# Linear attention and a feed-forward layer on one core: all tokens of k and v in five chunks instead of four chunks and a rest

## Chip, cores and metric

The kernel runs on one core of one Trainium2 chip. The metric is the device time in microseconds (us) of one execution, lower is better. Before the change it was 295.58 us (median of 3 runs, 295.31 to 296.41). Times of a kernel are compared with runs of the kernel before on the same chip. A run is called slow when it is more than 1.5% above the fastest of its kernel, and slow runs are left out of ratios; the medians and ranges quoted take in all runs.

## The reference

```python
# q, k, v: 8 batches, 8 heads, 576 tokens, 64; w_in 512 x 2048; w_out 2048 x 512; all float32
phi = lambda x: np.where(x > 0, x, np.exp(x) - 1.0) + 1.0
kv  = einsum('bhsd,bhse->bhde', phi(k), v);  z = sum over s of phi(k)
att = (phi(q) @ kv) / (phi(q) @ z + 1e-6)                  # per batch and head
x   = att as (8*576, 512);  out = gelu_tanh(x @ w_in) @ w_out
```

576 tokens don't divide into blocks of 128 partitions: 4 x 128 leave 64. How those 64 are treated is what changes.

## The kernel before

A batch's 512 main tokens are loaded as four chunks ("main"); the 64 others ("rest") of two batches share one tile of 128 partitions. So q, k and v have a main and a rest path each. Loads and DMA transposes are issued by SyncE (SP), the rest loads mostly by GpSimd (POOL).

```python
pld   = ctx.enter_context(tc.tile_pool(name="pld", bufs=6))    # staged float32 loads, one tag
...
psm = ctx.enter_context(tc.tile_pool(name="psm", bufs=2))      # transposed q of the rest
px  = ctx.enter_context(tc.tile_pool(name="px", bufs=5))       # attention output x, before its transpose
...
    def load_main(src, b, name, eng, parts=1):
        t = pld.tile([P, H, C * D], FP32, name=name, tag="ld")
...
        # five matmuls for each pair of heads: four main chunks, then the rest
        for c in range(C):
            nc.tensor.matmul(dst, lhsT=kp[:, c, ...], rhs=vps[b % 2][...], start=(c == 0), stop=False)
        nc.tensor.matmul(dst, lhsT=kr[:, 0, ...], rhs=vrs[...][...], start=False, stop=True)
...
    def plan_rest(m, j0, j1):
        def tq():
            box["qt"] = psm.tile([P, NP, P], BF16, name="qtr")
            nc.sync.dma_start_transpose(out=box["qt"], in_=phi["qr", m]...)
        def nab(): ...          # reads box["qt"], makes x, transposes x into xt_rest on SP
        at(*j0, tq); at(*j1, nab)
...
    plan_rest(1, (2, 2, 8), (1, 3, 14))
    for m in range(2, 4):
        at(1, 2 * m - 2, 9, lambda m=m: load_rests(m, (("qr", q),)))
    for m in range(2, 4):
        plan_rest(m, (2, 2 * m - 2, 9), (1, 2 * m, 14))
```

The program is laid out by hand in slots (half, stage, slot); every engine runs its own instructions in that order. The transpose of q's rest m=1 is placed at (2, 2, 8) and that of m=2 at (2, 2, 9), next to each other, and the first is read only much later.

## Time and profile before

| | before |
|---|---|
| time, median | 295.58 us |
| span of the profiled run | 293.4 us |
| TensorE (PE) busy | 285.2 us, 97% |
| first matmul of the feed-forward layer | 20.33 us |
| data moved by DMA in the first 60 us | 21.09 MB |
| all DMA traffic | 53.23 MB |

TensorE sets the time; what can cost time is whatever makes it wait. Two views matter for what follows and are not in the prediction. The first shows busy time of each engine in stretches, with the granted clock, the busy share of the DMA engines and GB/s as the last three numbers:

```profile
12.00:20.00 8.00, 6.63 (x77) 4.86 (x74) 5.93 (x17) 4.98 (x11) 2.16 (x3) 1.00 1.08 384
20.00:30.00 10.00, 9.85 (x67) 6.33 (x69) 6.19 (x9) 8.08 (x13) 5.26 (x6) 1.00 1.06 391
```

The columns after the length of the stretch are PE, PE's weight loads, DVE, ACT and POOL. Between 12 and 30 us the DMA engines are full (1.08 and 1.06) and move 384 and 391 GB/s. PE works 9.85 of the 10 us from 20 to 30.

The second is the timeline of SP's queue around 110 us: start, duration of the issue, line, what.

```profile
106.55 3.66 SPq L522 DMA_TRANSPOSE xt_rest<-x  x1
111.71 6.79 SPq L463 DMA_TRANSPOSE qt<-q_p  x4
118.55 2.63 SPq L512 DMA_TRANSPOSE qtr<-qr_p  x2
122.69 7.17 SPq L498 DMA_TRANSPOSE xt<-x  x4
```

One queue carries the transposes of q of batch 4, then those of two rests of q, then those of x, one behind another. The division that needs the first of them runs at 121.26 without a wait.

### The profile page before, as it was taken

To read this page: it belongs to the slowest core of one execution; us is meant where nothing else is said; L and a number is where in the kernel's file an instruction comes from. 1 tells how busy PE (TensorE), PEld (TensorE's weight loads), DVE (VectorE), ACT (ScalarE), POOL (GpSimd) and SP (SyncE) were. 2 spreads that over 40 slices of the span, in tenths; PEclk is the share of its full clock that TensorE was granted. 3 is DMA by queue.
4 is the path that set the end of the run, shared out by engine and by line. 5 is a ranking of instruction groups with operands and counts; after the bars stand their busy time and mean duration, and the time that the engine had idled before them with its cause. 6 is when DMAs were issued, how large, how long until landed. Compare 5 with 4: busy or idle time off the path is not lost.

```text
span 293.4 us, 4220 instructions
## 1 busy us (share of the span) xinstructions
PE 285.2 (97%) x1669; PEld 149.2 (51%) x1698; DVE 114.3 (39%) x189; ACT 158.6 (54%) x221; POOL 36.0 (12%) x56
## 2 busy tenths in 40 slices
PE   8989999999999999999999999999999999999995
PEld 6865456644565544544454445544554444444443
DVE  3676426236486683356125652543231000000002
ACT  4539943679965772567255935682560176017400
POOL 8045458400005200000000000000000000000000
PEclk9999999999999999999999999999999999999999
DMA  7999999994599899539914797304231110021032
GB/s 233 317 373 401 398 365 387 333 365 141 150 344 247 179 283 294 159 61 287 307 64 72 251 306 127 71 3 139 75 60 31 71 71 2 0 96 47 2 72 72
DMA packets 64259, 53.23 MB, mean 181 GB/s; under 512 B 31728, under 2 KB 57584, under 8 KB 64240
## 3 DMA queue, kind: packets, MB, share of 16 engines
q1 hardware_dynamic: 60816, 41.82, 51.1%
q10 hardware_dynamic: 2464, 8.52, 7.8%
q0 software_dynamic: 960, 2.62, 3.1%
q8 instruction: 13, 0.21, 0.3%
q14 instruction: 6, 0.05, 0.0%
HBM read 36.70 MB, written 9.44 MB: 157 GB/s over the span
## 4 chain that ended last, share of the span: by engine, by line
PE 91%; DMA 3%; DVE 3%; issue 1%; SPq 0%; ACT 0%; DVEq 0%
PE h_ps L309 42%; PE o_ps L727 40%; DMA q_x<-in_q_dram 3%; PE n_ps L261 3%; PE kv_ps L227 3%; PE o_ps L696 1%; PE t_ps L284 1%; DVE x L273 1%; DVE kvbd L250 1%; PE kv_ps L234 1%; SPq L67 0%; ACT q_e L168 0%; PE t_ps L255 0%; DVE xt L391 0%; DVE q_p L185 0%
## 5 line engine op out<-in xcount | busy, mean ns | idle before, releaser
L727 PE MATMUL o_ps<-w_out_sb,g 128*128 128x512 bf16 x547 | 123.4, 379 | 0.8 <-issue 0.2
L309 PE MATMUL h_ps<-xt,w_in_sb 128*128 128x512 bf16 (+1 forms) x534 | 118.6, 364 | 0.8
L684 ACT ACTIVATE g<-h_ps 128x512 bf16<-128x512 f32 x144 | 83.7, 602 | 46.6 <-PE h_ps L309 44.9
L727 PEld LDWEIGHTS <-g 128*128 128x128 bf16 x560 | 54.2, 98 | 62.6
L309 PEld LDWEIGHTS <-w_in_sb 128*128 128x128 bf16 x612 | 57.6, 97 | 54.7 <-issue 0.5
L742 ACT COPY o_sb<-o_ps 128x512 f32<-128x512 f32 x18 | 10.5, 585 | 57.8 <-PE o_ps L727 57.8
L740 DVE COPY o_sb<-o_ps 128x512 f32<-128x512 f32 x17 | 11.7, 688 | 64.5 <-PE o_ps L727 57.2
L273 DVE TENSOR_TENSOR x<-n_ps,r 128x512 bf16<-128x512 f32 x36 | 24.9, 691 | 1.2
L250 DVE CAST kvbd<-kv_ps 64x260 bf16<-64x260 f32 (+1 forms) x16 | 6.6, 410 | 39.5 <-PE kv_ps L234 39.4
L168 ACT ACTIVATE k_e<-k_x 128x2048 bf16<-128x2048 f32 (+1 forms) x9 | 15.5, 1721 | 4.7 <-DMA k_x<-in_k_dram 4.6
L168 ACT ACTIVATE q_e<-q_x 128x2048 bf16<-128x2048 f32 (+1 forms) x10 | 15.5, 1557 | 3.5 <-DMA q_x<-in_q_dram 3.5
L271 DVE RECIPROCAL r<-n_ps 128x8 f32<-128x8 f32 x36 | 7.4, 205 | 24.1 <-PE n_ps L261 24.1
L185 DVE TENSOR_TENSOR k_p<-k_p,k_e 128x2048 bf16<-128x2048 bf16 (+1 forms) x9 | 10.5, 1172 | 13.3 <-ACT k_e L168 13.2
L336 PE MATMUL w_ps<-warm 128*128 128x252 bf16 x94 | 13.8, 312 | 1.2 <-DVE warm L127 1.1
L309 PE MATMUL h_ps<-xt_rest,w_in_sb 128*128 128x512 bf16 x62 | 13.9, 379 | 0.1
L261 PEld LDWEIGHTS <-qt 128*128 128x128 bf16 x128 | 9.7, 98 | 7.9 <-issue 1.0
L211 DVE CAST vp<-v_x 128x2048 bf16<-128x2048 f32 (+1 forms) x9 | 9.3, 1042 | 11.0 <-DMA v_x<-in_v_dram 11.0
L261 PE MATMUL n_ps<-kvbd,qt 128*128 128x130 bf16 x128 | 12.7, 221 | 0.6 <-ACT kvbd L250 0.2
L179 DVE TENSOR_SCALAR q_p<-q_x 128x2048 bf16<-128x2048 f32 (+1 forms) x10 | 10.6, 1064 | 6.7 <-DMA q_x<-in_q_dram 6.5
L227 PEld LDWEIGHTS <-k_p 128*128 128x128 bf16 x128 | 9.6, 96 | 6.2 <-DVE vp L211 0.8
L227 PE MATMUL kv_ps<-vp,k_p 128*128 128x130 bf16 x128 | 11.8, 220 | 0.5 <-DVE vp L211 0.5
L336 PEld LDWEIGHTS <-warm 128*128 128x128 bf16 x94 | 10.4, 113 | 3.4 <-DVE warm L127 1.1
(52 smaller groups left out, 140.3 us busy)
## 6 DMA issues: line engine op xcount, KB each, us to landing
out_dram<-o_sb ACTq DMA_DIRECT2D x16, 512.0 KB, 4.9
k_x<-in_k_dram SPq DMA_DIRECT2D x7, 1024.0 KB, 5.9
v_x<-in_v_dram SPq DMA_DIRECT2D x7, 1024.0 KB, 12.1
q_x<-in_q_dram SPq DMA_DIRECT2D x6, 1024.0 KB, 8.6
w_st<-in_moe_w_out_dram SPq DMA_DIRECT2D x4, 1024.0 KB, 11.1
w_st<-in_moe_w_in_dram SPq DMA_DIRECT2D x3, 1024.0 KB, 8.6
q_x<-in_q_dram SPq DMA_DIRECT2D x4, 512.0 KB, 10.0
k_x<-in_k_dram SPq DMA_DIRECT2D x2, 512.0 KB, 4.2
```

The costliest lines, as they stand in the source:

```text
L168: nc.scalar.activation(e[:, :, hs, :].rearrange("p c h d -> p h c d"), by_chunk(x[:, hs]), AF.Exp)
L179: nc.vector.tensor_scalar(xp[:, :, hs, :].rearrange("p c h d -> p h c d"), by_chunk(x[:, hs]), 1.0, 1.0, op0=ALU.add, op1=ALU.max,)
L185: nc.vector.tensor_tensor(xp[:, :, hs, :], xp[:, :, hs, :], e[:, :, hs, :], op=ALU.min)
L227: nc.tensor.matmul(dst, lhsT=kp[:, c, P * i : P * (i + 1)], rhs=vps[b % 2][:, 2 * i : 2 * i + 2, c, :], start=(c == 0), stop=False,)
L261: nc.tensor.matmul(n_ps[rows, i // 2, 2 * E * (i % 2) : 2 * E * (i % 2) + 2 * E], lhsT=qt_c[:, i, rows], rhs=kvbd[:, i, :], skip_group_che ...
L273: nc.vector.tensor_tensor(x, n_v[:, :, :, 0:D], r[:, :, :, None].to_broadcast([P, 2, 4, D]), op=ALU.mult,)
L309: nc.tensor.matmul(h_ps[:, tok], lhsT=w_in_sb[:, c, P * m : P * (m + 1)], rhs=xt[:, c, tok], start=(c == 0), stop=(c == KM - 1), skip_grou ...
L336: nc.tensor.matmul(w_ps[:, 0:252], lhsT=warm[:, 0:P], rhs=warm)
L684: nc.scalar.activation(gs[j][:, i, :], ps, AF.Gelu_apprx_tanh)
L727: nc.tensor.matmul(o_pss[t], lhsT=g[:, m, P * t : P * (t + 1)], rhs=w_out_sb[:, m, :], start=(m == 0), stop=(m == MM - 1),)
L740: nc.vector.tensor_copy(dst, o_ps)
L742: nc.scalar.copy(dst, o_ps)
```

## The change

The intent: the rest path of k and v goes away. All 576 tokens of k and v are laid out in five chunks: even partitions take five of nine consecutive tokens, odd ones four. The fifth chunk of the odd partitions is filled with zeros and masked in phi(k). That removes the 256-byte rest loads of k and v and their small instructions, and keeps 160 matmuls of the same shape. q keeps its rest. To make room (the fifth chunk makes load tiles 10,240 bytes per partition instead of 8,192), two rings lose a buffer.

```diff
-    psm = ctx.enter_context(tc.tile_pool(name="psm", bufs=2))
-    px = ctx.enter_context(tc.tile_pool(name="px", bufs=5))
+    psm = ctx.enter_context(tc.tile_pool(name="psm", bufs=1))
+    px = ctx.enter_context(tc.tile_pool(name="px", bufs=4))
...
+    def load_kv(src, b, name, parts=1, fill=nc.gpsimd):
+        t = staged(name, LD).rearrange("p (h x) -> p h x", h=H)
+        for i in range(parts):
+            s = slice(i * hs, (i + 1) * hs)
+            fill.memset(t[:, s, C * D :], 0.0)
+            x = src[b, s].rearrange("h (r n) d -> r h (n d)", n=2 * C + 1)
+            nc.sync.dma_start(out=t[1:P:2, s, 0 : C * D], in_=x[:, :, CK * D :])
+            nc.sync.dma_start(out=t[0:P:2, s], in_=x[:, :, 0 : CK * D])
...
-    vps = [const.tile([P, H, C, E], BF16, name=f"vp{i}") for i in range(2)]
-    vrs = [ ... four tiles [P, H, E] ... ]
+    even = const.tile([P, 1], FP32, name="even")
+    vps = [const.tile([P, H, CK, E], BF16, name=f"vp{i}") for i in range(2)]
...
+            nc.vector.scalar_tensor_tensor(          # phi_min, fifth chunk
+                xp[:, C, hs, :], xp[:, C, hs, :], even, e[:, C, hs, :],
+                op0=ALU.mult, op1=ALU.min)
...
-        for c in range(C):  ... stop=False;  then the matmul of the rest, stop=True
+        for c in range(CK): ... stop=(c == CK - 1)
...
-        at(2, 2 * m - 3, 3, lambda m=m: load_rests(m, (("kr", k), ("vr", v))))
-        at(1, 2 * m - 2, 9, lambda m=m: load_rests(m, (("qr", q),)))
+        at(1, 2 * m - 2, 9, lambda m=m: load_rest(m, nc.gpsimd))
```

Cut: the removed helpers of the rests of k and v, the same edits in the prologue, and batch 3's load, which moves behind the first rest loads.

## The prediction

> **What bounds the kernel now.** I read the page from the top: part 1 (busy time), then the groups by line for the instructions that the change touches, then the chain that ended last in order of time, then the timeline of the first 20 us.
>
> ```profile
> span 293.4 us, 4220 instructions
> PE 285.2 (97%) x1669; PEld 149.2 (51%) x1698; DVE 114.3 (39%) x189; ACT 158.6 (54%) x221; POOL 36.0 (12%) x56
> ...
> L227 PE MATMUL kv_ps<-vp,k_p 128*128 128x130 bf16 x128 | 11.8, 220 | 0.5 <-DVE vp L211 0.5
> ...
> L234 PE MATMUL kv_ps<-vr,kr_p 128*128 128x130 bf16 x32 | 7.0, 218 | 0.0
> ```
>
> PE works 97% of the span; DVE, ACT and POOL have 179, 135 and 257 us to spare. The work that the change merges is the last two rows: four matmuls over main chunks plus one over the rest for each of 32 pairs of heads, 160 in all. Five chunks make 32 x 5 = 160 matmuls of the same shape. So the bound engine gets no work and loses none.
>
> Busy time of PE is modelled, so I checked it by pitch in the chain:
>
> ```profile
> 2.34 9.05 DMA q_x<-in_q_dram
> ...
> 12.50 0.69 DVE q_p L185
> 13.19 0.34 DVE kr_p L179
> ...
> 13.97 0.41 DVE vr L219
> 14.38 0.33 DVE qt L345
> 14.71 0.35 DVE vp L211
> ...
> 174.60 1.73 PE h_ps L309 x8
> ```
>
> Columns: start, us, what. Eight 512-column matmuls take 1.73 us, 216 ns each, back to back. Between 145 and 235 us PE is busy 14.89 to 14.95 of each 15 us that I cut. What is left to win is only where the chain is not PE: the first 20 us (q's loads until 11.39, then ACT, DVE, small matmuls), a DVE eviction of about 0.9 us at 46.2, a copy of 0.4 us at 53.5, and some 3 us of last copies and stores.
>
> The first matmul of the MLP starts at 20.33 us. What leads there:
>
> ```profile
> 0.83 0.16 DVE L127 MEMSET warm<- 128x126 uint32 x1 [0.83 <-PEq L787]
> ...
> 1.06 10.63 PE L336 MATMUL w_ps<-warm 128*128 128x252 bf16 x72 [1.06 <-DVE warm L127]
> ...
> 11.53 0.61 PE L344 MATMUL t_ps<-ident,q_p 128*128 128x128 bf16 x8
> ...
> 13.25 0.64 PE L344 MATMUL t_ps<-ident,q_p 128*128 128x128 bf16 x8
> ...
> 14.30 0.41 DVE L345 COPY qt<-t_ps 128x512 bf16<-128x512 bf16 x1
> 14.31 1.25 ACT L211 CAST vp<-v_x 128x512 bf16<-128x512 f32 x2
> ```
>
> Two things end together here: the data of q (second half landed 11.39) and PE's own queue of 72 warming matmuls, which is issued to its end just when the first half of q is ready. PE takes them in order, so nothing of q can be transposed before the 72 are through.
>
> **What the Trainium skill says.** "TensorE: Matmul & The Clock Gate", Part 1: the array starts at half rate and a free-running window of 3.4 us must be busy before it runs at full rate. The trace agrees in kind: until about 7.0 us the warming matmuls come roughly every 0.21 us (252 columns), afterwards every 0.107 us. It means that a later start of them costs a cold matmul's worth less than its delay. "VectorE: DVE Perf Modes", Zero memsets can be issued as uint32: a memset takes one cycle per element whatever the type. 126 words took 163 ns here, which fits one cycle at 0.96 GHz plus some 30 ns. "DMA: Bandwidth & Descriptors", Specifications: 512 B is the minimum for line rate. The rest loads have 256 B runs; the trace agrees: while the two of the prologue are in flight (9 to 11 us) the engines are full (share 1.16 and 1.14) but move 192 and 260 GB/s, against 354 at 7 to 8 us and 376 at 12 to 13. The same page, Rules for kernel authors, says of two transfers to disjoint partition halves that they serialize on the same 16 engines and gain nothing. A pair for odd and even partitions is that; no run here shows its price yet.
>
> **The change, part by part.**
>
> Bytes: five chunks of 9 tokens in 128 partitions are the 576 tokens, so the same bytes in 1280 B and 1024 B runs. Each k or v load becomes two issues of half the descriptors. On SP an issue of 512 KB took about 0.5 us, one of 1024 KB 0.91 us, so it goes by descriptors and two halves cost one whole.
>
> Steady state, per batch (durations by shape, the slope from the 1024 and 2048 forms). ACT: exp of k goes from 2048 to 2560 elements, 512 x 0.83 ns = +0.43, less half a rest exp, 0.61/2 = -0.31: +0.12 us. DVE: line of phi 512 x 0.51 = +0.26, the masked minimum of the fifth chunk, estimated at one element a cycle, +0.60, cast of v +0.26; less half of a rest line (0.42), of a rest minimum (0.43) and of two rest casts (0.84): -0.84. Sum +0.28 us, some 2 us in all on an engine 39% busy. POOL: twelve rest issues of 0.69 us go (8.2 us), and 14 fills of 512 elements come, estimated 0.6 to 1 us each. All lies beside PE: 0.
>
> Early middle, 20 to 66 us, where DMA is full (share 1.05 and over): v of batch 1 lands at 42.85, its cast ends at 44.1 and PE takes it at 44.80, 0.7 us of slack. The bytes ahead of it are the same, with less in 256 B runs: not later. The even half of k of batch 2 must now wait for a fill that stands on POOL behind the cast of the third piece of w_out (ends 42.1). A backlog until 45.4 (the fourth piece landing) hides that. Batch 3 is asked for at about 50 us instead of 46; 3.4 MB for batch 2, then 3.4 MB for batch 3 at 0.38 MB/us: done near 66 us, wanted near 75. The rings of x (5 to 4) and of the rest's q (2 to 1) are reused only several slots later. Nothing on the path: 0.
>
> Prologue. (a) Removed from the chain: the kr and vr work on DVE between 13.19 and 14.38. It cannot all be won: the copy of qt after it needs the transposes, done at 13.9, so it is worth 0.4 us. (b) Added: DVE does four fills of 256 floats before it clears the tile of the warming matmuls. 256/0.96 + 30 = 0.30 us each, about 1.1 us together. The warming starts at 2.1 instead of 1.06; by 7.0 us it has done 23 instead of 28, so it ends at about 7.0 + 49 x 0.107 = 12.2 us; at 12.7 if the clock opens a full delay later. Transposes of the first half then at 12.3, ten more warming matmuls that stand in the program between the two halves (1.07), transposes of the second half from about 13.8 (now 13.25), copy of qt on DVE from 14.5 (now 14.30). (c) ACT loses a rest exp (0.61), but its third copy waits for that later transpose, then come two casts of v with 640 elements, 0.72 us each instead of 0.62: the second ends near 16.2 instead of 15.56. The last pair of kv needs it: +0.35 to +0.7 us by the time kv is complete, after which the rest of the chain is the same. (d) q: 131 KB of k are now ahead of it, +0.35 us at 370 GB/s, against the 256 B loads no longer crowding it. It may land from 9.5 to 11.8; either way PE's queue, through the second half's transposes near 13.8, hides it (11.8 + 1.07 + 0.69 = 13.6).
>
> Sum: 0 in the steady state, about +0.4 us in the prologue.
>
> **The rivals.** First, that the prologue gets faster: q and v land up to 2 us earlier without the 256 B loads, and the DVE chain is shorter. For it: the dip of GB/s above. Against: the warming queue in front of the transposes. If the fills take half of my figure, it would be 295.58 - 0.5 to - 1.0, about 294.8. Second, that strided half loads run slower, or use the engines unevenly: from 20 to 66 us DMA is the resource without slack, v of batch 1 has 0.7 us of it. At 10% lower rate that load (some 40 us of full DMA) comes 3 to 4 us late and PE waits 3 us: 299. Against: both halves spread over the whole of the partitions, with runs of 1 KB or more. Third, a POOL fill that blocks an in-order queue, so that a load misses its slot: 1 to 2 us, about 297; my slacks of several us speak against it.
>
> **Range and chances.** 295.58 + 0.4 = 296.0, say 295.9, as the first rival is likelier than the second. Three runs before spread over 1.1 us. The two prologue readings give 294.8 to 296.6; with the spread 294.5 to 297.4. Within 2% means 289.7 to 301.5: faster would need 5.9 us out of 8.2 us in which PE idles at all, mostly start and end; slower needs the second rival in full force.
>
> **What would show it.** Right: 160 kv matmuls in one group, PE busy within 1 us of 285, first MLP matmul at 20.5 to 21.2 us, warming from about 2.1, the rest of the chain unbroken at 216 ns. Wrong: warming from under 1.6 us and the first MLP matmul before 20.0 (first rival); PE waiting at kv of batch 1 for the cast of v (second); DVE or ACT waiting for k or v of batches 2 to 7 with PE idle behind them (third).

## The result, and the profile after

After the change the time is 309.53 us (median of 4 runs, 306.24 to 310.15), before 295.44 beside it. The ratio is 1.045 (95% interval 1.037 to 1.053): slower. Ratios here are the mean time of one kernel's fast runs over that of the other's of the same rounds, so they are not quite the ratio of the medians quoted.

The page of the changed kernel, top lines:

```profile
span 307.2 us, 4256 instructions
...
PE 288.4 (94%) x1669; PEld 149.6 (49%) x1698; DVE 115.7 (38%) x185; ACT 159.7 (52%) x216; POOL 32.1 (10%) x49
```

PE's busy time rose by 3.2 us only, with the same 1669 instructions; the span rose by 13.8. So nearly 11 us are idle time of PE, and the rest is slower clock. The waits of PE, as total, number and longest in us:

```profile
PE n_ps L251 <- DMA qt<-q_p: 6.8, 2, 4.3
PE w_ps L323 <- DVE warm L135: 2.1, 1, 2.1
PE kv_ps L224 <- DVE vp L214: 1.5, 2, 1.0
PE o_ps L696 <- POOL w_out_sb L162: 0.7, 1, 0.7
PE h_ps L299 <- ACT g L653: 0.6, 1, 0.6
```

The first line is new and the largest: twice PE stands still for a transposed q. Where the loss arises, by comparing starts of the same matmuls in the two traces:

| PE reaches | before | after | later by |
|---|---|---|---|
| first feed-forward matmul | 20.33 | 20.75 | 0.4 |
| second block of h | 53.92 | 55.96 | 2.0 |
| output of stage 2 | 103.05 | 106.23 | 3.2 |
| output of stage 3 | 130.59 | 139.92 | 9.3 |
| output of stage 4 | 160.79 | 174.46 | 13.7 |

So there is a small early loss of 3 us and then two jumps of 6.2 and 4.3 us. The early part, by stretches:

```profile
12.00:20.00 8.00, 6.57 (x82) 5.20 (x81) 5.64 (x14) 4.97 (x9) 1.36 (x2) 1.00 1.07 364
20.00:30.00 10.00, 9.15 (x68) 5.80 (x67) 5.40 (x8) 7.13 (x10) 4.71 (x5) 1.00 1.05 369
```

The DMA engines are as full as before (1.07, 1.05) but move 364 and 369 instead of 384 and 391 GB/s. Full engines that move less are the first sign that each byte has become dearer, not that less is asked for. In the first 60 us 19.81 MB are moved instead of 21.09.

SP's queue at the first jump:

```profile
111.43 5.66 SPq L496 DMA_TRANSPOSE xt_rest<-x  x1
117.18 9.24 SPq L438 DMA_TRANSPOSE qt<-q_p  x4
126.53 13.67 SPq L486 DMA_TRANSPOSE qtr<-qr_p  x2
140.30 2.52 SPq L472 DMA_TRANSPOSE xt<-x  x2
```

The four transposes of q take 9.24 us of issue, 6.79 before, and land after 11.67. The two of q's rest take 13.67, 2.63 before: the second waits for its only buffer, which the first division of a rest gives free at about 139. Everything behind it in the queue, x first of all, is 17.6 us later than before. POOL's queue just ahead of that:

```profile
113.18 0.53 POOL L88 MEMSET v_x<- 128x512 f32 x1 [5.43 <-issue]
113.71 1.49 POOL L97 DMA_DIRECT2D q_r<-in_q_dram  x2
```

The last rest load of q, issued at 95.58 before, now stands behind fills that wait for a free load tile, and is issued at 113.71, straight into the transposes. PE, with its idle time in brackets:

```profile
128.90 0.41 PE L251 MATMUL n_ps<-kvbd,qt 128*128 128x130 bf16 x4 [4.29 <-DMA qt<-q_p]
...
129.84 2.77 PE L299 MATMUL h_ps<-xt,w_in_sb 128*128 128x512 bf16 x6 [0.22 <-issue]
```

After the stall six matmuls take 2.77 us, 462 ns each instead of 216: the granted clock is 0.50 from 130 to 132 us. That is 1.5 us more, so the stall of 4.3 us costs about 5.8 of this jump's 6.2 us.

The second jump holds a stall of the same kind:

```profile
163.49 0.62 PE L251 MATMUL n_ps<-kvbd,qt 128*128 128x130 bf16 x4 [2.55 <-DMA qt<-q_p]
```

The transposes that it waits for are issued at 154.07 us, 139.93 before, as they stand behind the delayed part of SP's queue. Here too the granted clock is 0.50 afterwards, from 164 to 166 us.

### The profile page after: what moved, and what is told of

Same layout as the page of the kernel before. It is cut to its first block, busy times and chain, and to the rows that moved or that the text cites. A ratio compares the mean times of both kernels' runs of the same rounds, so it can differ in the third digit from the quotient of the medians.

```text
span 307.2 us, 4256 instructions
## 1 busy us (share of the span) xinstructions
PE 288.4 (94%) x1669; PEld 149.6 (49%) x1698; DVE 115.7 (38%) x185; ACT 159.7 (52%) x216; POOL 32.1 (10%) x49
## 3 DMA queue, kind: packets, MB, share of 16 engines
q0 software_dynamic: 384, 1.05, 1.6%
## 4 chain that ended last, share of the span: by engine, by line
PE 74%; DMA 16%; DVE 3%; SPq 2%; issue 2%; POOL 1%; ACT 1%; DVEq 0%
PE o_ps L696 35%; PE h_ps L299 31%; DMA qt<-q_p 7%; DMA w_st<-in_moe_w_in_dram 4%; PE n_ps L251 3%; DMA w_st<-in_moe_w_out_dram 3%; DMA q_x<-in_q_dram 2%; PE kv_ps L224 2%; SPq L91 1%; PE o_ps L665 1%; SPq L90 1%; POOL w_in_sb L155 1%; DVE vp L214 1%; PE t_ps L274 1%; DVE kvbd L240 1%
## 5 line engine op out<-in xcount | busy, mean ns | idle before, releaser
L299 PE MATMUL h_ps<-xt,w_in_sb 128*128 128x512 bf16 (+1 forms) x534 | 121.6, 371 | 1.6 <-ACT g L653 0.6
L299 PEld LDWEIGHTS <-w_in_sb 128*128 128x128 bf16 x612 | 58.3, 99 | 57.3 <-issue 3.7
L174 ACT ACTIVATE k_e<-k_x 128x2560 bf16<-128x2560 f32 (+1 forms) x9 | 18.9, 2101 | 7.6 <-DMA k_x<-in_k_dram 7.5
L214 DVE CAST vp<-v_x 128x2560 bf16<-128x2560 f32 (+1 forms) x9 | 11.4, 1268 | 13.6 <-DMA v_x<-in_v_dram 13.6
L323 PE MATMUL w_ps<-warm 128*128 128x252 bf16 x94 | 13.1, 302 | 2.1 <-DVE warm L135 2.1
L224 PEld LDWEIGHTS <-k_p 128*128 128x128 bf16 x160 | 11.1, 97 | 7.4 <-issue 1.3
L224 PE MATMUL kv_ps<-vp,k_p 128*128 128x130 bf16 x160 | 13.2, 220 | 1.5 <-DVE vp L214 1.5
L185 DVE TENSOR_SCALAR k_p<-k_x 128x2560 bf16<-128x2560 f32 (+1 forms) x9 | 12.1, 1339 | 4.5 <-DMA k_x<-in_k_dram 4.5
```

Of the source, the lines that this page charges most:

```text
L174: nc.scalar.activation(e[:, :, hs, :].rearrange("p c h d -> p h c d"), by_chunk(x[:, hs]), AF.Exp)
L185: nc.vector.tensor_scalar(xp[:, :, hs, :].rearrange("p c h d -> p h c d"), by_chunk(x[:, hs]), 1.0, 1.0, op0=ALU.add, op1=ALU.max,)
L214: fn(out=vps[b % 2][:, s, :, 0:D], in_=ld["v", b][:, s].rearrange("p h (c d) -> p h c d", d=D),)
L224: nc.tensor.matmul(dst, lhsT=kp[:, c, P * i : P * (i + 1)], rhs=vps[b % 2][:, 2 * i : 2 * i + 2, c, :], start=(c == 0), stop=(c == CK - 1),)
L299: nc.tensor.matmul(h_ps[:, tok], lhsT=w_in_sb[:, c, P * m : P * (m + 1)], rhs=xt[:, c, tok], start=(c == 0), stop=(c == KM - 1), skip_grou ...
L323: nc.tensor.matmul(w_ps[:, 0:252], lhsT=warm[:, 0:P], rhs=warm)
```

## The experiments

Eighteen kernels ran. Five theories are named in the expectations. A: the smaller rings (one buffer for the transposed rest of q, four for x). B: loads of k and v as two half loads. C: the late rest load, which meets the transposes of q. D: the staged tiles land in other slots, so that the weights wait. E, formed late: the addresses of the tiles. (In the expectation of e7 "Theory E" still means something else, the wait for the cast of v.)

### e1 to e5: undoing and doing parts

**e1**: the change, with both rings given back. The rest's transposed q is put into its later place, since two buffers don't fit.

```diff
-    psm ... bufs=1;  px ... bufs=4
+    px ... bufs=5
-            box["qt"] = psm.tile([P, NP, P], BF16, name="qtr")
+            box["qt"] = xt_rest[:, :, P * m : P * (m + 1)]
```

> The changed kernel with its lost buffers given back: the transposed q of the rest is kept in its own block of xt_rest (so no ring of one buffer is left), and x has five buffers again. Theory A (the one-buffer ring: its second transpose waits 13.7 us in SP's queue for the reader of the first, holds the transposes of x, the loads of batch 6 and so the second stall): the stall at 154 to 164 us goes, DVE no longer waits 3.6 us for x, 309.5 falls by 4 to 5 us to about 305; the stall at 124 to 129 stays, since it is before that wait. Rival B (both stalls come from the pairs of loads and the fills in SP's and POOL's queues): nothing changes by more than 1 us.

Measured: 304.87 us (303.81 to 307.71), ratio 1.031. The second stall is gone, the first stays at 4.3 us.

**e2**: e1, and the last rest load of q (m = 3) asked for earlier.

```diff
-        at(1, 2 * m - 2, 9, lambda m=m: load_rest(m, nc.gpsimd))
+        at(1, 2, 9, lambda m=m: load_rest(m, nc.gpsimd))
```

> As the run with the buffers back, and the last rest load of q (batches 6 and 7) is issued beside that of batches 4 and 5, at about 95 us as in the kernel before, not at 113.7 us where POOL reaches it behind two fills. Theory C (the first stall, 124 to 129 us, comes from this load, whose 256-byte pieces share the engines with the transposes of q of batch 4): that stall of 4.3 us and its 1.5 us of slow clock go, about 299. Rival B (the loads of batch 5 themselves are late and slow, as five issues instead of three): the stall stays within 1 us, the time within 1 us of the run with the buffers back.

Measured: 299.15 us (298.51 to 299.62), ratio 1.010. No wait for a transposed q is left.

**e3**: the kernel before, with only the two rings cut (psm 2 to 1, px 5 to 4).

> The kernel before with only its rings shrunk as in the change: one buffer for the rest's transposed q, four for x. Theory A: the same wait in SP's queue appears (about 10 us before the second of the two transposes near 120 us), loads of batch 6 come 10 us late and PE stalls once: 298 to 302. Rival (the short rings only hurt where the loads are late anyway): 295 to 296.5.

Measured: 300.28 us (297.16 to 302.01, the last of them slow), ratio 1.011 (1.002 to 1.019). The two transposes of the rest take 12.77 us of SP's queue there, and PE waits 2.4 us for a transposed q near 154 us. So the rings cost some 1% by themselves.

**e4**: the kernel before, with its main loads of k and v split into odd and even partitions.

```diff
+                for s in (1, 0):
+                    eng.dma_start(out=t[s:P:2, ...], in_=x[s:P:2])
```

> The kernel before with each main load of k and v split into a load of the odd and one of the even partitions, the same bytes and no fill. Theory B (pairs of issues delay SP's queue and the starting loads): loads start about 0.7 us poorer in the first 10 us, the first MLP matmul or the casts of w_in come 0.5 to 1.5 us later, and the transposes behind the loads of batch 5 come about 2 us later: 297 to 300. Rival: pairs cost nothing but issue time that is hidden: 295 to 296.

Measured: 295.92 us, ratio 1.0005 (0.994 to 1.007). Theory B falls. The first four issues of half the partitions took 2.78 us of SP's queue, where the two whole ones of the kernel before took 1.01, but the data came as fast: 389 GB/s from 20 to 40 us against 384.

**e5**: the change, with only the earlier rest load of e2, rings as changed.

> The changed kernel with only the rest load of q for batches 6 and 7 moved back to about 95 us; rings as in the change. If the two stalls have two causes that add: stall one (124 to 129 us) gone, stall two (154 to 164) still there behind the 10 us wait of the second rest transpose, about 309.5 - 6 = 303 to 304. If the second stall was only an echo of the first: about 299.

Measured: 302.9 us (301.39 to 303.25), ratio 1.023. The first stall is gone, the second stays. Together with e1 this shows two stalls with two separate cures, 4.7 and 6.6 us of the 309.5.

### e6 to e8: what is left after e2

**e6**: e2 with every staged tile pinned to the slot that it has in the kernel before.

```diff
+    slots = iter((0, 5, 4, 1, 2, 3, 0, 5, 4, 1, 3, 2, ...))
-        return pld.tile([P, LD], FP32, name=name, tag="ld")[:, 0:width]
+        return pld.tile([P, LD], FP32, name=name, tag=f"ld{next(slots)}")[:, 0:width]
```

> As e2 (rings back, rest load early), and each staged tile is put by hand into the slot that the kernel before used for it, so that the first piece of w_out no longer waits for the cast of the second piece of w_in (issued at 26.2 us in e2, 20.65 in the kernel before). Theory D (the 1 to 2 us that PE loses from 20 to 45 us come from that wait): no PE wait for a cast of w_in or w_out, 1 to 1.5 us less, about 298. Rival (they come from the lower rate of the loads, 369 to 375 GB/s against 385 to 391 in all kernels of the old form): within 0.5 us of e2.

Measured: 298.56 us, ratio 1.010. PE still waited 2.1 us for the cast of a piece of w_out. The issue of the first w_out no longer waits for a slot (19.49 us, 26.16 in e2), but the data come late all the same, and the ratio is that of e2: theory D explains about 0.6 us at most.

**e7**: e6 with kv of batch 3 one slot later, behind its cast of v (`(7, 8, 9, 10)` becomes `(8, 9, 10, 11)`).

> As e6, and the kv matmuls of batch 3 are placed one step later in the first half. Theory E (PE waits 1.0 us there for the cast of v, since k of 2560 elements, the masked minimum of 0.74 us and the wider cast stand in front on DVE): that wait goes, 0.8 to 1 us less than e6. Rival: the wait moves on to the matmuls that read kv: no gain.

Measured: 298.23 us, ratio 1.008. The wait for v's cast shrank from 1.5 to 0.5 us, the time by 0.3 only.

**e8**: e7 with the clearing of the warming tile before the fills on DVE, so that PE warms up at 1.1 us again.

> As e7, and DVE clears the tile of the warming matmuls before it fills the four pieces of k and v, so that they start at 1.1 us, not 2.1. My prediction's step (b): the first MLP matmul comes 0.3 to 0.5 us earlier. Rival (q's data is the later of the two, as PE waited for q in the profile of e2): no gain beyond 0.2 us.

Measured: 297.68 us (297.18 to 298.48), ratio 1.007. PE then waited 2.2 us for q's phi instead: the first feed-forward matmul came no earlier (20.95 us, 20.87 in e7). The rival was right.

### e9 to e12: is it the rest load?

**e9**: the kernel before, with its rest loads of m = 3 moved to other slots and that of q held by a one-element copy on POOL, which waits for the cast v of batch 4.

```diff
+    tick = const.tile([P, 1], BF16, name="tick")
...
+    at(1, 2, 10, lambda: load_rests(3, (("kr", k), ("vr", v))))
+    at(2, 2, 4, lambda: nc.gpsimd.tensor_copy(out=tick, in_=vps[0][:, 0, 0, 0:1]))
+    at(2, 2, 4, lambda: load_rests(3, (("qr", q),)))
```

> The kernel before with one thing moved: the rest load of q for batches 6 and 7 is held on POOL until the cast of v of batch 4 is done, so that it is issued at about 108 us (96 us before), some 3 us ahead of the transposes of q of batch 4, as in the changed kernel. Theory C: the first of those transposes lands late, PE waits for it 2 to 4.5 us near 121 us and runs slowly for a while after: 298 to 301. Rival (the load only hurts when the loads of batch 5 are late and in pairs as well): no PE wait for that transpose, 295 to 296.5.

Measured: 303.5 us (301.49 to 303.93), ratio 1.024. Slower than theory C asks (298 to 301), and in the wrong place: PE had lost 3 us already by 35 us, long before the held load.

**e10**: the kernel before with only the rest's ring cut (psm 2 to 1).

> The kernel before with one buffer for the rest's transposed q, but five for x as it had. If the single buffer alone makes the second stall: the same as the run with both rings short (300.3, at least 298). If the ring of x is needed for it: 295 to 296.5.

Measured: 300.86 us (299.69 to 301.18), ratio 1.017. PE waits 2.9 us for a transposed q near 156 us, behind the same held queue:

```profile
120.09 12.17 SPq L512 DMA_TRANSPOSE qtr<-qr_p  x2
```

The single buffer alone makes the second stall. Not all of the 1.7% need be its doing: in the profiled run PE also waited 1.2 us for q's phi near 12 us, and the first feed-forward matmul came at 21.07 us.

**e11**: e9 made cleaner: all loads keep their places, only the last rest load of q is held.

```diff
+        if m == 3:
+            at(1, 4, 9, lambda: nc.gpsimd.tensor_copy(out=tick, in_=vps[0][:, 0, 0, 0:1]))
```

> The kernel before with one thing more: POOL copies one element of the cast v of batch 4 just before it issues the last load of q's rest, so that this load goes at about 110 us, when batch 4's v is cast, instead of 95.6; all other loads keep their places and slots. Theory C (the 256-byte rest load beside the transposes of q is what makes them late): the four transposes of q of batch 4, issued from 111.7, take 9 us or more instead of 6.8, the division of batch 4's first block (121.3 in before) waits for them 0.5 to 3 us, and the time is 296.5 to 299. Rival (the transposes are slow for other reasons, such as the main loads with two halves): they keep 6.8 us and the time stays 295.3 to 296.

Measured: 302.66 and 303.81 us in its two fast runs, two more at 313 that count as slow. Again the loss was there from the start: from 20 to 30 us PE worked 8.14 of 10 us, at 335 GB/s. The four transposes did take 9.13 us, as theory C asks, and PE waited 1.6 us for them.

**e12**: the change, with its last rest load issued from ACT's queue.

```diff
+        at(1, 2 * m - 2, 9, lambda m=m: load_rest(m, (nc.gpsimd, nc.scalar)[m - 2]))
```

> The kernel after, with the last load of q's rest issued from ACT's queue behind the tenth gelu of its stage (about 128 us) instead of from POOL's behind the two fills (113.7): later than in after, but when the transposes of q of batch 4 are through. Theory C: those transposes (9.2 us of issue in after, landed after 11.7) take 7 us or less again, PE's wait of 4.3 us for qt at 128.9 is gone or below 1 us, at the price of two issues on ACT (0.3 to 0.7 us each, a gelu later by about 1 us); second stall stays: 303 to 305. Rival (not this load but the loads of batch 5 just ahead of the transposes make them late): the wait stays above 3 us and the time is 308 to 311.

Measured: 302.62 us (302.44 to 303.84), ratio 1.026. I had misjudged the place: ACT issued it at 161.9 us, not 128. SP's queue:

```profile
115.89 6.73 SPq L438 DMA_TRANSPOSE qt<-q_p  x4
```

6.73 us instead of 9.24, and no first stall. Earlier (e5) or later (e12), the same gain: in the changed kernel it is the meeting of that load with the transposes which makes the first stall.

### e13 to e18: the addresses

e9 and e11 slowed the first 30 us, where nothing of their edit runs. What they do share with the changed kernel is one more small tile among the constants. The compiled program lists where each tile lies in SBUF. Tiles are packed in order, each rounded up to 32 bytes, so a small tile moves all those behind it. In the kernel before, the targets of all loads lie on multiples of 256 bytes. In e9 and e11 they lie 32 past one. In the changed kernel (larger vp tiles, no vr tiles, the 4-byte mask) the sum of the constants is smaller by 2,080 bytes, 8 x 256 + 32, and the targets lie 224 past one. So do those of e1, e2, e5 to e8 and e12; e3, e4 and e10, made from the kernel before, keep 0.

**e13**: the change, with the mask's tile 64 bytes wide. No instruction differs; the targets come back to multiples of 256.

```diff
-    even = const.tile([P, 1], FP32, name="even")
+    even = const.tile([P, 16], FP32, name="even")[:, 0:1]
```

> The kernel after, with the small tile of the mask made 64 bytes wide instead of 4, so that every tile behind it in SBUF starts 32 bytes later: on a multiple of 64, as in before; in after all targets of loads start at 32 past one. No instruction changes. Theory E (misaligned targets are what slows the loads of after): rates of 12 to 20, 20 to 30 and 30 to 40 us rise from 364, 369, 374 to 380 or more, the two waits for w_out (0.6 and 0.7 us) shrink, the time is 306 to 308.3 with both late stalls still there. Rival (1280-byte runs, pairs or fills): rates and time as in after, 308.5 to 310.

Measured: 299.67 us median (298.68, 299.55, 299.80, and one slow run of 305.31), before 294.75; ratio of the fast runs 1.015 (1.011 to 1.019). Against the kernel before beside it, some 9 us of the 14 came back from 32 bytes in these three runs. The gain is larger than expected, which assumed that the late stalls stay. The profiled run is the slow one, whose early part is comparable all the same, as its loads run from the same program:

```profile
12.00:20.00 8.00, 6.61 (x82) 5.38 (x82) 5.54 (x14) 4.49 (x10) 1.96 (x2) 1.00 1.07 393
20.00:30.00 10.00, 9.74 (x69) 6.22 (x68) 5.15 (x8) 8.28 (x12) 5.66 (x7) 1.00 1.04 386
```

393 and 386 GB/s, at the same busy share, and PE works 9.74 of 10 us. In that slow run PE waits 5.9 us for transposed q, much as in the changed kernel. The fast runs are 6.0 us shorter on average; they have no trace, so that they are free of these waits is only argued. The slow run is no run at an odd clock either (0.994, as in many fast runs): one run in four of this kernel still has the stalls, so moved targets don't remove them for certain.

**e14**: the reverse, the kernel before with 32 bytes added behind the tile of the warming matmuls. No instruction differs.

```diff
-    warm = const.tile([P, 252], BF16, name="warm")
+    warm = const.tile([P, 268], BF16, name="warm")[:, 0:252]
```

> The kernel before, with 32 bytes more behind the tile of the warming matmuls, so that every later tile starts 32 past a multiple of 64; no instruction changes. Theory E: the rates of 12 to 20 and 20 to 30 us fall from 384 and 391 to 330 to 365, PE waits 2 to 4 us in all for q's phi, w_in's and v's casts in the first 50 us, the time is 298 to 301. Rival (addresses do not matter): 295.2 to 296.

Measured: 304.75 us (303.93 to 305.98), ratio 1.033 (1.029 to 1.037). The same stretches, and the waits of PE:

```profile
12.00:20.00 8.00, 5.83 (x67) 4.26 (x65) 5.39 (x15) 4.70 (x10) 1.06 (x2) 1.00 1.08 358
20.00:30.00 10.00, 7.84 (x62) 5.34 (x64) 6.28 (x9) 6.26 (x9) 4.58 (x4) 1.00 1.09 327
```

```profile
PE n_ps L261 <- DMA qt<-q_p: 3.9, 3, 1.8
PE h_ps L309 <- POOL w_in_sb L149: 1.9, 1, 1.9
PE kv_ps L227 <- DVE vp L211: 1.7, 3, 0.8
PE w_ps L336 <- DVE warm L127: 1.1, 1, 1.1
PE o_ps L727 <- POOL w_out_sb L156: 1.0, 1, 1.0
```

Of these lines only the warming (1.1 us) stands in before with that size. The weights and v arrive late, PE waits for their casts, and then three times for q's transposes. A kernel with not one instruction changed loses 10.0 us against the 294.75 us beside it.

**e15**: e11 with its tile at 64 bytes (`tick` of 32 elements), so all later tiles are shifted by 64.

> The kernel of e11 with its one-element tile made 64 bytes, so that all later tiles keep their alignment of before. Theory C and E: the early part is as in before (first MLP matmul near 20.3), the held load goes at 108 to 110 us, the four transposes of q of batch 4 take 8.5 us or more (6.8 in before), the division at 121 waits 0.5 to 3 us for them: 296.5 to 299. Rival to C: transposes 6.8 us, time 295.2 to 296.

Measured: 299.88 us (298.40 to 301.79), ratio 1.017. My belief that a multiple of 64 is enough fell: the first 30 us are slow again (361 and 346 GB/s, PE waits 2.7 us for w_in), while nothing waits for q's transposes.

**e16**: e8 with e13's edit: both sides mended.

> The kernel of e8 with the mask's tile at 64 bytes, so that the loads' targets are aligned as in before. Theory E: e8's 297.7 falls by 1 to 2 us to 295.7 to 296.7, rates at 12 to 40 us above 380; the wait of 2.2 us for q's phi shrinks. Rival: stays at 297.2 to 298.2.

Measured: 296.76 us (6 runs, 296.12 to 298.78), before 294.75; ratio 1.008 (1.004 to 1.012). The loads ran at 392 and 403 GB/s, and PE's wait for q's phi fell from 2.2 to 0.7 us. The median lies between the two expectations, and the ratio is that of e8 (1.007), as the rival has it. Once the stalls are gone, faster loads win nothing that shows. This and e8 are the best versions with the change; neither beats the kernel before.

**e17**: e14 with 128 bytes (`warm` of 316 elements).

> As e14, but with 128 bytes instead of 32: the load targets lie 128 past a multiple of 256. Theory E in its sharper form (a target must start on a multiple of 256): rates of 12 to 20 and 20 to 30 us fall below 365 as in e14 and e15, PE waits 2 us or more for the cast of w_in near 28 us, 298 to 305. Rival (a multiple of 128 is enough): 295.2 to 296.2.

Measured: 298.80 us (297.08 to 299.72), before 296.15; ratio 1.010 (1.003 to 1.017). The rates fell as in e14 and e15 (362 and 356 GB/s); PE's wait for w_in's cast was 1.1 us, not 2 or more. A multiple of 128 is not enough.

**e18**: e11 with its tile at 256 bytes (`tick` of 128 elements): a shift that keeps every place within 256, and the rest load still held.

> As e15, but with the one-element tile made 256 bytes, so that every later tile is shifted by a whole 256 and keeps its place within 256. Theory E: the first 50 us are as in before, rates 384 and 391, no wait for w_in: a shift as such costs nothing. Theory C: the held load goes at about 110 us and the transposes of q of batch 4 (issued from about 112) take 7.5 us or more instead of 6.8; PE then waits up to 2 us for them at 121: 295.5 to 298. Rival to C: no wait for qt, 295.2 to 296.

Measured: 295.19 us (294.52 to 295.63), ratio 0.997 (0.991 to 1.003). Its early stretches, then the held load in POOL's timeline, then the transposes in SP's:

```profile
12.00:20.00 8.00, 6.56 (x77) 4.83 (x76) 6.32 (x17) 4.62 (x10) 2.51 (x3) 1.00 1.08 387
20.00:30.00 10.00, 9.72 (x64) 5.82 (x63) 5.32 (x7) 7.58 (x11) 4.92 (x6) 1.00 1.06 385
```

```profile
109.09 2.06 POOL L76 DMA_DIRECT2D q_r<-in_q_dram  x2 [0.55 <-issue]
```

```profile
111.96 7.74 SPq L463 DMA_TRANSPOSE qt<-q_p  x4
```

A shift as such is harmless. The load now stands 2.9 us ahead of the transposes (3.5 in the changed kernel), and they take 7.74 us instead of 6.79, which the slack of this kernel hides. So theory C is no cause by itself: it needs a schedule whose slack is already spent. The other traces show that load and address both count: these four transposes take 6.1 to 6.9 us with targets at 0 and no late load, 7.7 to 8.1 with it (e13, e18); at 224 past, 6.7 to 7.1 and 9.1 to 9.2 (e1, after); at 32 past, 8.0 (e14) and 9.1 to 9.4 (e9, e11).

The runs by address:

| kernel | targets of loads past a multiple of 256 | GB/s, 12 to 20 and 20 to 30 us | MB in the first 60 us | ratio to before |
|---|---|---|---|---|
| before | 0 | 384, 391 | 21.09 | 1 |
| e18, before + 256, load held | 0 | 387, 385 | 21.07 | 0.997 |
| e17, before + 128 | 128 | 362, 356 | 19.80 | 1.010 |
| e15, before + 64, load held | 64 | 361, 346 | 19.23 | 1.017 |
| e14, before + 32 | 32 | 358, 327 | 18.95 | 1.033 |
| after | 224 | 364, 369 | 19.81 | 1.045 |
| e13, after, aligned (profile of its slow run) | 0 | 393, 386 | 21.06 | 1.015 |
| e8, order mended | 224 | 365, 379 | 20.01 | 1.007 |
| e16, order mended, aligned | 0 | 392, 403 | 21.50 | 1.008 |

Of the seven kernels at 0 that ran, six have moved 21 MB by 60 us; the seventh is e10, whose profiled run started late (20.6 MB). The thirteen others have moved 20.0 MB or less.

The single packets in the traces say it more directly, and for e10 too. In the first 60 us every kernel moves the same 3584 packets of 2048 bytes. On average one takes 84.3 to 86.7 ns in the seven kernels at 0 and 88.7 to 91.0 ns in the thirteen others. The packets of 1024 bytes take 50.2 ns in the kernel before, 54.6 at 128 past, 55.7 at 64 and 56.6 at 32 (e17, e15, e14); in the changed kernel 51.4, aligned (e13) 47.9. Work on the engines doesn't slow down with the address: the exp of 2048 elements of k takes 1910 ns before and 1911 in e14, the cast of v 1222 in both. So the address acts through the transfers.

## Why the prediction was wrong

The prediction of 295.9 us, with a range of 294.5 to 297.4, was wrong: 309.53 us. Two of its steps failed.

**First failed step: "The bytes ahead of it are the same, with less in 256 B runs: not later."** It took the rate of the loads as given by bytes and run length. The change moved every tile behind the constants, and with that the start of every target. Rates fell by 5 to 6% (364 and 369 against 384 and 391 GB/s), and v of batch 1, which the step is about, landed at 44.79 us instead of 42.85 (43.06 in e13). With targets moved back (e13) the kernel regains some 9 us in three of four runs; with targets moved away (e14) the kernel before loses 10.0. The Trainium skill has a section on this that I should have drawn on: "DMA: Bandwidth & Descriptors", How a descriptor splits into AXI transactions. It says that a transaction must start on a multiple of 256 bytes, so that a descriptor which doesn't start there begins with a transaction from the boundary below, whose unused bytes still cost beats (units of 32 bytes). It speaks of bytes fetched; whether the same holds for the target of a load, it doesn't say. The runs agree on the boundary: shifts by 32, 64 and 128 are slow, by 256 not. They show rates and times only, not the transactions. If its count held for targets, 1024 bytes would take 32 beats aligned, 33 from 32 bytes past a boundary and 36 from 128 past (an estimate from that section's rule). The runs have the other order: 32 past (56.6 ns a packet, ratio 1.033) was dearer than 128 past (54.6, 1.010).

**Second failed step: "The rings of x (5 to 4) and of the rest's q (2 to 1) are reused only several slots later. Nothing on the path: 0."** I looked at who reads and writes each ring, not at who stands behind it. Two transposes of q's rest stand next to each other in SP's in-order queue, with one buffer between them. The second blocks x's transposes and all loads behind it. e10 shows 1.7% with that ring alone cut, e3 1.1% with both (the intervals overlap), on the kernel before with the targets of its loads unmoved.

**The third rival was the right kind, in the wrong place.** A POOL fill that blocks an in-order queue was named, for 1 to 2 us, and dismissed by slacks of several us. The slack of the main loads was indeed enough. What the fills delayed, by 18 us, was the rest load of q, which then met the transposes: first stall, 4.3 us of wait and some 6 of time (e5, e12). But e18 shows the same meeting without loss.

The two late stalls nearly add: moving the load (e5) gains 6.6 us, the rings (e1) 4.7, both (e2) 10.4. The addresses don't add to them: alone (e13) they gain some 9 us, after e2's kind of mending nothing (e8 and e16). I read this as one loss with two conditions: dearer transfers used up the slack, and the tighter order of queues turned lateness into stalls of PE, with a slow clock after each. Removing either condition removes most of it, the first not in every run. In e14 the dearer transfers alone were enough.

Point by point, the rest of the prediction:

- PE's work: 160 matmuls of kv, as predicted. PE's busy time was to be within 1 us of 285 and came to 288.4; part of that is the slow clock after stalls, in which matmuls took 462 ns and not "unbroken" 216.
- Prologue: warming predicted at 2.1 us, measured 2.15, with its 72 matmuls through at 12.12 (12.2 predicted); first feed-forward matmul predicted at 20.5 to 21.2, measured 20.75. The fills of 256 elements took 0.27 us each, 0.30 estimated. The numbers are right, the path is partly luck: q was to be hidden by PE's queue, but its halves landed at 10.59 and 12.10 us (9.5 to 11.8 predicted), the phi of the first was ready at 12.40, and PE waited 0.33 us for it. e8 confirms that q was the later of the two.
- "two halves cost one whole" for SP's issues: wrong, each half took 0.61 to 0.77 us in the first microseconds, a whole one about 0.5 before. In e4 this cost nothing.
- Second rival, slower strided halves: wrong as a cause (e4), though its sign, a rate down by some per cent, was seen. In e16 the same strided halves ran at 392 and 403 GB/s: it was the address, not the stride.
- DVE: "All lies beside PE: 0". Nearly: work that the kernel before did a batch earlier now stands before kv of batch 3, 1.0 us of PE's wait (line kv_ps above). Moved in e7, it gave 0.3 us. The masked minimum took 0.745 us (0.60 estimated), a fill of 512 elements on POOL mostly 0.53 (0.6 to 1 estimated).
- Range: it had no place for a change that moves every buffer; "slower" was left to "the second rival in full force". It stood on a sum of instruction times; that part was nearly right and told little.

What stays open: 0.7 to 0.8% between e8 or e16 and before; why 32 bytes past a boundary is the worst of the places tried; which of the moved tiles (targets of loads, sources of transposes and stores) carries how much, since all moved together; and what decides between the fast runs of e13 and its slow one.

## What to carry to other kernels

When a change adds, drops or resizes any small tile, look up where the large DMA targets land, and keep them on multiples of 256 bytes, the only places that were fast here; a wider small tile does it. Where full DMA engines suddenly move fewer GB/s over the same traffic, check addresses as well as strides. Before cutting a ring to one buffer, look at what stands behind its next writer in the same in-order queue, not only at its readers. And a control experiment that adds a tile has changed more than it says: pad it so that nothing else moves.

## What the Trainium skill lacked or had wrong

- "DMA: Bandwidth & Descriptors", How a descriptor splits into AXI transactions: it has the 256-byte boundary, but no rule for authors and no price follows. Here 32 bytes of shift took the rate from 391 to 327 GB/s (20 to 30 us) and the kernel from 294.75 to 304.75 us. It doesn't say whether its count of beats holds for the targets of loads; if it does, it gives the wrong order: 32 past a boundary cost 3.3%, 128 past it 1.0%.
- The same page, DMA Transpose (X-bar), Constraints, asks for 32-byte alignment in SBUF. Every run here kept to that and was correct, and none broke it; but it says nothing of speed: the four transposes took 8.00 us at 32 past a multiple of 256 (e14), 6.79 before, and a reader may take 32 as enough. (In e14 other traffic is slower too, so this is not the price of the transposes' own addresses.)
- No page has a price for DMA transposes that are issued 3 us behind loads with 256-byte runs: 7.74 us of issue for four (e18) instead of 6.79, 9.24 in the changed kernel.
- No page has the issue time of half loads: 0.61 to 0.77 us for 64 partitions, where 512 KB over 128 partitions took about 0.5.
